# A decode block's last sum in two halves on GpSimd and VectorE, its x written by VectorE, and Wo's rows in other pieces

## Chip, cores and metric

The kernel runs on one core of one Trainium2 chip. Its time is in microseconds (us) of device time; the median of three runs before the change is 197.61 us (197.59 to 197.65). One execution was also recorded by the hardware profiler; all stage times and durations are from it.

## What is computed

One decoding step for eight sequences: a layer norm of x, attention of 32 query heads over the last 2,048 positions of a cache with 8 key and value heads, and beside it a gated unit whose result scales the attention's output.

```python
x = A_x                                    # 8 x 1 x 512
xn = layernorm(x)
W = min(4096, max(256, Sk // 4))           # 2048 of 8192
q = xn @ wq                                # 32 heads of 128
k, v = last W positions of the caches, each head for 4 query heads
p = softmax(q k * 128 ** -0.5)
s = (p v) @ wo                             # 4096 -> 512
h = sigmoid(xn @ w_gate) * (xn @ w_up)     # 512 -> 1792
g = silu(h @ w_down)                       # 1792 -> 512
return x + s * g
```

All inputs are bf16. Keys, values and weights are about 81 MB, each byte used once.

## The kernel before

**Loads.** All large loads are issued from SyncE's queue, in one list `loads` (L156 to L162): Wq, then keys and values of the eight sequences in turn, then the gate and up weights, the down weights and Wo. Each goes into one of five equal buffers (`ring`); `issue_loads` (L165) issues as many as there are free buffers and is called again whenever the code has put down the last use of one. A load into a used buffer waits on SyncE's queue for the engines that read the buffer. Each DMA also takes one of eight completion lanes in turn and waits until the lane's earlier DMA has landed.

**x.** ScalarE's queue loads x once as `x_bf`, 8 partitions of 512 (L84). For the last sum x is also wanted in another layout, `x2_sb`: columns 0 to 255 on partitions 0 to 7, columns 256 to 511 on partitions 32 to 39, zeros in the rest (L94). `load_x2` (L121), in the list behind sequence 3's first value load, makes it: GpSimd copies the first half from `x_bf` (L122), and a DMA from SyncE fetches the second half from memory (L123). It needs no ring buffer.

**Start.** VectorE does the layer norm; PE transposes it; VectorE copies it to `xnT_sb` (L210). From L213 on VectorE makes small constants from the identity, and GpSimd copies them into larger ones (L222 to L299) and clears `qz` and `o2_sb` (L305, L377). PE computes the queries (L316).

**Loop over sequences.** VectorE transposes the keys in four pieces (`k_turn`, L384), PE computes scores (L401), VectorE and ScalarE the softmax, PE spreads the probabilities (L447) and multiplies them with the values (L501), and the result goes to `o2_sb` (L552).

**End.** The gated unit (L569 to L610) leaves `gate`, 64 x 256, in the same two-part layout. Wo is loaded in pieces by rows (`load_wo`, L141): 128 partitions with 32 rows of 512 each, rows 0 to 30 in pieces of 11, 8, 6, 4 and 2 (L147) and row 31 in two halves of columns (L153). PE goes through the rows in order (`out_row`, L676), two matmuls for each of the two column halves `s`, into two PSUM tiles. After row 31's half `s` VectorE multiplies that half with `gate` into `prod` (L690). When both halves are there, one VectorE operation adds `x2_sb` (L694) and two DMAs, one each from SyncE and ScalarE, write the two halves of the columns to memory (L696).

Of the kernel before, what the change touches and what calls it, by code (L numbers as in the profile page):

```python
# [10 lines left out]
def kernel(  # L11
# [13 lines left out]
    nc = tc.nc  # L25
    P = 128
    B, _, D = A_x.shape
# [22 lines left out]
    NCOL = 2  # L50
    DC = D // NCOL
# [6 lines left out]
    bf16 = mybir.dt.bfloat16  # L58
# [3 lines left out]
    ALU = mybir.AluOpType  # L62
# [5 lines left out]
    work = ctx.enter_context(tc.tile_pool(name="work", bufs=1))  # L68
# [14 lines left out]
    x_bf = work.tile([B, D], bf16, name="x_bf")  # L83
    nc.scalar.dma_start(out=x_bf[:], in_=A_x.flatten_outer_dims())  # L84

    def ring_tile(name):
        return ring.tile([P, BIG], bf16, name=name, tag="ring", align_bytes=ALIGN)
# [5 lines left out]
    x2_sb = work.tile([NCOL * 32, DC], bf16, name="x2_sb")  # L93
# [24 lines left out]
        v_tiles[b] = t  # L118
        load_heads(t, A_v_cache, b)

    def load_x2():  # L121
        nc.gpsimd.tensor_copy(out=x2_sb[:B, :], in_=x_bf[:, :DC])  # L122
        nc.sync.dma_start(  # L123
            out=x2_sb[32 : 32 + B, :], in_=A_x.flatten_outer_dims()[:, DC:]
        )

    def load_in():
        t = ring_tile("wgu_sb")
        for n, w in enumerate((B_w_gate, B_w_up)):
            v = t[:, n * KT * F : (n + 1) * KT * F].rearrange(  # L130
                "p (kt n) -> p kt n", kt=KT
            )
            nc.sync.dma_start(out=v, in_=w.rearrange("(p kt) n -> p kt n", kt=KT))
            w_tiles["gu"[n]] = v
# [7 lines left out]
    def load_wo():  # L142
        t = ring_tile("wo_sb")
        v = t[:].rearrange("p (m n) -> p m n", m=MR)
        src = A_wo.rearrange("(p m) n -> p m n", m=MR)
        for m0, m1 in ((0, 11), (11, 19), (19, 25), (25, 29), (29, 31)):
            nc.sync.dma_start(out=v[:, m0:m1, :], in_=src[:, m0:m1, :])  # L147
        last, last_src = (
            w[:, MR - 1, :].rearrange("p (c s n) -> p s c n", c=NCOL, s=2)
            for w in (v, src)  # L150
        )
        for s in range(2):
            nc.sync.dma_start(out=last[:, s], in_=last_src[:, s])  # L153
        w_tiles["o"] = v

    loads = [(load_wq,), (load_k, 0), (load_k, 1), (load_k, 2), (load_v, 0)]  # L156
    for b in range(3, B):
        loads += [(load_k, b), (load_v, b - 2)]
        if b == 3:
            loads.append((load_x2,))  # L160
    loads += [(load_v, B - 2), (load_v, B - 1), (load_in,), (load_down,), (load_wo,)]
    free_bufs = [RING]  # L162

    def issue_loads():
        while loads:  # L165
            small_one = loads[0][0] is load_x2
            if not small_one and free_bufs[0] == 0:
                return
            f, *a = loads.pop(0)
            f(*a)  # L170
            if not small_one:
                free_bufs[0] -= 1

    issue_loads()


# [14 lines left out]
        out=rstd[:], in_=mv[:, 1:2], func=AF.Sqrt, bias=eps_t[:], scale=1.0  # L191
# [4 lines left out]
        out=xn_bf[:],  # L196
        in0=x_f[:],
# [6 lines left out]
    for kt in range(KT):  # L204
        nc.tensor.transpose(
            out=xnT_ps[:, kt, :], in_=xn_bf[:B, kt::KT], identity=ident[:B, :B]
        )
    xnT_sb = work.tile([P, KT, PW], bf16, name="xnT_sb")
    nc.vector.memzero(xnT_sb[:])
    nc.vector.tensor_copy(out=xnT_sb[:, :, :B], in_=xnT_ps[:])  # L210

    rows16 = consts.tile([P, GR], f32, name="rows16")
    nc.vector.tensor_reduce(  # L213
        out=rows16[:],
        in_=ident[:].rearrange("p (g x) -> p x g", x=GR),
        axis=AX.X,
        op=ALU.add,
    )
    rows128 = []
    for gg in range(NG):  # L220
# [3 lines left out]
            out=t[:, :, gg],  # L224
            in_=rows16[:]
# [8 lines left out]
        out=quarter[:],  # L234
        in_=ident[:].rearrange("p (h q) -> p q h", q=QP),
        axis=AX.X,
        op=ALU.add,
    )
    nc.gpsimd.tensor_copy(
        out=block[:], in_=quarter[:].unsqueeze(2).to_broadcast([P, QP, PW])  # L240
# [3 lines left out]
        out=same[:],  # L244
        in_=ident[:].rearrange("p (g j r) -> p g r j", j=QP, r=rep),
        axis=AX.X,
        op=ALU.add,
# [3 lines left out]
        out=SumM[:].rearrange("p (g j r) -> p g j r", j=QP, r=rep),  # L251
        in_=same[:]
# [6 lines left out]
        out=Jneg[:],  # L259
        in_=ident[:].rearrange("p (a j r) -> p j a r", j=QP, r=rep),  # L260
        axis=AX.XY,
        op=ALU.add,
    )
    nc.vector.tensor_scalar(
        out=Jneg[:], in0=Jneg[:], scalar1=-scale, scalar2=None, op0=ALU.mult
# [3 lines left out]
        out=Hm[:],  # L269
        in_=ident[:].rearrange("p (a gl) -> p gl a", gl=GL),  # L270
        axis=AX.X,
        op=ALU.add,
# [3 lines left out]
        out=Cm4[:],  # L276
        in_=ident[:].rearrange("p (u c x) -> p c u x", c=4, x=GR),
        axis=AX.XY,
        op=ALU.add,
# [3 lines left out]
        out=Cm2[:],  # L283
        in_=ident[:].rearrange("p (u c x) -> p c u x", c=2, x=GR),
        axis=AX.XY,
        op=ALU.add,
# [3 lines left out]
        out=heads[:], in_=same[:].unsqueeze(2).to_broadcast([P, XR, QP])  # L290
# [3 lines left out]
        out=spr[:],  # L294
        in_=ident[:].rearrange("k (gl cl p) -> k cl p gl", gl=GL, cl=CL),
    )
    quad = consts.tile([P, QP, QP, PW], bf16, name="quad")
    for a in range(QP):
        nc.gpsimd.tensor_copy(  # L299
            out=quad[:, :, a, :], in_=ident[:].rearrange("k (a w) -> k a w", a=QP)  # L300
# [10 lines left out]
    for s in range(2):  # L311
# [13 lines left out]
        for e in range(2):  # L325
            nc.vector.tensor_copy(  # L326
                out=qx_sb[:, s, :, :, e, :],
                in_=q_ps[:].rearrange(
                    "p (r wb w e) -> p e r wb w", r=rep, wb=WE // 2, e=2
                )[:, e],  # L330
            )
    free_bufs[0] += 1
    issue_loads()
    qT_sb = work.tile([P, 2 * rep * WE, PW], bf16, name="qT_sb")
    nc.vector.transpose(
        out=qT_sb[:].rearrange("p m b -> p (m b)"),
        in_=qx_sb[:].rearrange("p s r wb e w -> p (s r wb e w)"),
    )
    qc_sb = work.tile([P, GL, NG, rep, WE, B], bf16, name="qc_sb")
    for i in range(2):  # L340
        qr_ps = psum.tile([P, 2, 2 * rep * WE * B], f32, name="qr_ps", tag="o_ps")
        for aa in range(2):
# [9 lines left out]
            out=qc_sb[:, 2 * i : 2 * i + 2].rearrange("p gl g r we b -> p (gl g r we b)"),  # L352
            in_=qr_ps[:].rearrange("p a m -> p (a m)"),
# [260 lines left out]
    for b in range(B + 1):  # L614
        s = b - 1
# [24 lines left out]
        if turn:  # L640
            qk(b)
            free_bufs[0] += 1
            issue_loads()
            if s - 1 >= 0:
                for gg in range(NG):
                    pv(s - 1, gg)
        else:
            pv(s - 1, 1)
# [23 lines left out]
    prod = work.tile([NCOL * 32, DC], bf16, name="prod")  # L672

    def out_row(m, s):
        for c in range(NCOL):
            nc.tensor.matmul(  # L676
                a_ps[s][32 * c : 32 * (c + 1), :],
                lhsT=o2_sb[:, m, :],
                rhs=w_tiles["o"][:, m, DC * c + HC * s : DC * c + HC * (s + 1)],
                start=(m == 0),  # L680
                stop=(m == MR - 1),
                tile_position=(0, 32 * c),
                skip_group_check=True,
            )

    for m in range(MR):
        for s, n in enumerate(halves):
            out_row(m, s)
            if m == MR - 1:
                nc.vector.tensor_tensor(  # L690
                    out=prod[:, n], in0=gate[:, n], in1=a_ps[s][:], op=ALU.mult
                )
    y_bf = work.tile([NCOL * 32, DC], bf16, name="y_bf")
    nc.vector.tensor_tensor(out=y_bf[:], in0=prod[:], in1=x2_sb[:], op=ALU.add)  # L694
    for c in range(NCOL):
        queues[c].dma_start(  # L696
            out=out.flatten_outer_dims()[:, DC * c : DC * (c + 1)],
            in_=y_bf[32 * c : 32 * c + B, :],
# [31 lines left out]
```

## Time and profile before

| | |
|---|---|
| median of runs | 197.61 us |
| profiled execution | 197.44 us |
| span of its instructions | 195.7 us |
| PE busy | 111.6 us (57%) |
| VectorE (DVE) busy | 117.6 us (60%) |
| ScalarE (ACT) busy | 38.6 us (20%) |
| GpSimd (POOL) busy | 6.4 us (3%) |
| read from memory | 81.01 MB, 414 GB/s over the span |
| TensorE clock granted, mean | 0.813 |

Busy times are sums over an engine's instructions; engines work side by side, so they don't add up to the span. The last landing of a large load is at about 192.3 us of the span, the last arithmetic at 193.06 to 193.34, the two output DMAs are issued at 193.37. The profiled execution is 0.17 us shorter than the median of the runs and 1.74 us longer than its own span.

The first use of GpSimd is at 0.24 us, the last one ends at about 11.5 us, with the copy for `x2_sb`.

### The profile page before, as it was taken

The numbers are of one execution on the slowest core, as the hardware profiler recorded it, in microseconds if no ns is written. First come the engines' busy times: TensorE is split into PE (matmuls) and PEld (weight loads), VectorE is DVE, ScalarE is ACT, GpSimd is POOL, SyncE is SP. The second block draws the span as 40 slices with busy tenths as digits, with TensorE's granted clock in tenths as the row PEclk, the third lists the DMA queues.
The fourth block names the chain that finished last, engine by engine and source line by source line (L and its number), as shares of the span: only waits on it lengthen the run. The fifth ranks groups of instructions, "written<-read, shape, count | busy, mean of one in ns | idle before, by whom it ended". The sixth has DMA issues, their size and how long they took to land.

```text
span 195.7 us, 2620 instructions
## 1 busy us (share of the span) xinstructions
PE 111.6 (57%) x1092; PEld 44.6 (23%) x1092; DVE 117.6 (60%) x176; ACT 38.6 (20%) x112; POOL 6.4 (3%) x22
## 2 busy tenths in 40 slices
PE   0133025709809980799059914990796199684362
PEld 0011001102002240214022411150215024462351
DVE  3404498299299449935895489739936952455001
ACT  3001910015015011501141104211501110233000
POOL 2730000000000000000000000000000000000000
PEclk9999555966985996589757985699589669999998
DMA  6999999999999999999999999999999999999991
GB/s 241 457 408 442 432 429 429 429 432 425 429 429 429 427 429 429 432 424 439 432 439 422 439 435 435 429 432 425 432 429 429 425 429 429 429 431 429 416 396 41
DMA packets 6410, 81.17 MB, mean 415 GB/s; under 512 B 992, under 2 KB 1024, under 8 KB 1408
## 3 DMA queue, kind: packets, MB, share of 16 engines
q1 hardware_dynamic: 6368, 81.01, 97.2%
q8 instruction: 8, 0.13, 0.2%
q10 hardware_dynamic: 32, 0.01, 0.0%
q14 instruction: 2, 0.02, 0.0%
HBM read 81.01 MB, written 0.01 MB: 414 GB/s over the span
## 4 chain that ended last, share of the span: by engine, by line
PE 38%; DVE 35%; DMA 23%; ACT 1%; issue 1%; SPq 1%; DVEq 0%
PE s_ps L401 27%; DVE k_sb L384 27%; DMA wo_sb<-in_A_wo_dram 12%; DMA k_sb<-in_A_k_cache_dram 11%; PE o_ps L501 8%; DVE pt_bf L441 2%; DVE o_r L522 2%; PE o_ps L530 1%; DVE o_sb L552 1%; ACT o_r L518 1%; DVE o_q L543 1%; DVE mx L414 1%; PE a_ps L676 1%; SPq L147 0%; SPq L101 0%
## 5 line engine op out<-in xcount | busy, mean ns | idle before, releaser
L384 DVE STREAM_TRANSPOSE k_sb<-k_sb 128x2048 uint32<-128x2048 uint32 x32 | 72.9, 2291 | 5.7 <-DMA k_sb<-in_A_k_cache_dram 5.7
L401 PE MATMUL s_ps<-k_sb,qz 128*32 128x512 bf16 x256 | 61.6, 1086 | 11.8 <-DVE k_sb L384 11.5
L447 PE MATMUL pc_ps<-pt_bf,spr 128*32 128x128 bf16 x128 | 4.7, 292 | 40.7 <-DVE pt_bf L441 40.7
L414 DVE TENSOR_REDUCE mx<-s_ps 128x1 f32<-128x512 f32 x8 | 5.5, 691 | 29.0 <-PE s_ps L401 29.0
L501 PE MATMUL o_ps<-v_sb,pT_sb 128*32 128x256 bf16 (+1 forms) x416 | 21.0, 298 | 0.0
L401 PEld LDWEIGHTS <-qz 128*32 128x32 bf16 x256 | 8.8, 115 | 49.8 <-issue 49.7
L501 PEld LDWEIGHTS <-pT_sb 128*32 128x32 bf16 (+1 forms) x416 | 14.0, 101 | 14.5 <-issue 9.9
L362 ACT COPY qz<-qc_sb 32x64 bf16<-32x64 bf16 x64 | 16.4, 302 | 0.7
L518 ACT ACTIVATE o_r<-o_ps,Cm 128x128 f32<-128x128 f32 x16 | 5.9, 368 | 52.0 <-PE o_ps L501 52.0
L522 DVE SCALAR_TENSOR_TENSOR o_r<-o_ps,Cm,o_r 128x128 f32<-128x128 f32 x28 | 9.7, 350 | 9.8 <-ACT o_r L518 9.3
L428 ACT ACTIVATE p_bf<-s_ps,nm 128x512 bf16<-128x512 f32 x8 | 5.5, 687 | 49.7 <-DVE nm L425 49.7
L447 PEld LDWEIGHTS <-spr 128*32 128x32 bf16 x128 | 3.4, 121 | 41.4 <-issue 40.7
L530 PE MATMUL o_ps<-o_r,rows 128*128 128x128 f32 x32 | 7.5, 320 | 4.8 <-DVE o_r L522 4.8
L483 DVE TENSOR_SCALAR pT_sb<-pc_bf,Hm 128x512 bf16<-128x512 bf16 x32 | 9.0, 352 | 0.2 <-ACT pc_bf L457 0.2
L457 ACT CAST pc_bf<-pc_ps 128x512 bf16<-128x512 f32 x8 | 4.7, 586 | 20.3 <-PE pc_ps L447 20.3
L316 PE MATMUL q_ps<-wq_sb,xnT_sb 128*32 128x512 bf16 x32 | 3.8, 626 | 6.8 <-DMA wq_sb<-in_A_wq_dram 6.5
L676 PE MATMUL a_ps<-wo_sb,o_sb 128*32 128x128 bf16 x128 | 4.6, 219 | 3.9 <-DMA wo_sb<-in_A_wo_dram 3.9
L530 PEld LDWEIGHTS o_ps<-o_r,rows 128*128 128x128 f32 x32 | 4.8, 189 | 6.7 <-DVE o_r L522 6.7
L326 DVE CAST qx_sb<-q_ps 128x256 bf16<-128x256 f32 x4 | 1.5, 420 | 7.7 <-PE q_ps L316 7.7
L441 DVE STREAM_TRANSPOSE pt_bf<-p_bf 128x512 bf16<-128x512 bf16 x8 | 5.4, 675 | 0.9 <-ACT p_bf L428 0.9
L543 DVE SCALAR_TENSOR_TENSOR o_q<-o_ps,rden,block 128x128 f32<-128x128 f32 x8 | 2.8, 351 | 4.7 <-PE o_ps L530 4.7
L690 DVE TENSOR_TENSOR prod<-gate,a_ps 64x128 bf16<-64x128 f32 x2 | 0.5, 279 | 7.5 <-PE a_ps L676 7.5
(64 smaller groups left out, 56.2 us busy)
## 6 DMA issues: line engine op xcount, KB each, us to landing
k_sb<-in_A_k_cache_dram SPq DMA_DIRECT2D x8, 4096.0 KB, 29.9
v_sb<-in_A_v_cache_dram SPq DMA_DIRECT2D x8, 4096.0 KB, 23.4
wq_sb<-in_A_wq_dram SPq DMA_DIRECT2D x1, 3072.0 KB, 11.6
wgu_sb<-in_B_w_gate_dram SPq DMA_DIRECT2D x1, 1792.0 KB, 25.1
wgu_sb<-in_B_w_up_dram SPq DMA_DIRECT2D x1, 1792.0 KB, 28.9
wd_sb<-in_B_w_down_dram SPq DMA_DIRECT2D x1, 1792.0 KB
wo_sb<-in_A_wo_dram SPq DMA_DIRECT2D x1, 1408.0 KB
wq_sb<-in_A_wq_dram SPq DMA_DIRECT2D x1, 1024.0 KB
```

The lines of the kernel that those rows point to most:

```text
L362: nc.scalar.copy(out=z[rows, GL * gg : GL * (gg + 1), :, c0 : c0 + rep], in_=qc_sb[rows, :, gg, :, :, b].rearrange("p gl r we -> p gl we r"),)
L384: nc.vector.transpose(out=words, in_=words)
L401: nc.tensor.matmul(s_tiles[b][PW * gl : PW * (gl + 1), :], lhsT=qz[b % 2][:, h, we, :], rhs=kv[:, gg, gl, we // 2, we % 2], start=(we == 0 ...
L414: nc.vector.reduce_max(out=mx[:], in_=s_tiles[b][:], axis=AX.X)
L441: nc.vector.transpose(out=pt_bf[:].rearrange("p c g a r -> p (c g a r)"), in_=p_bf[:])
L447: nc.tensor.matmul(pc_ps[PW * a : PW * (a + 1), cl], lhsT=spr[:, cl].rearrange("k p gl -> k (p gl)"), rhs=pt_bf[:, :, :, a, :], start=True ...
L483: nc.vector.tensor_scalar(out=pT[:, :, :, gl, :], in0=pc[:].rearrange("p c g r -> p g c r"), scalar1=Hm[:, gl : gl + 1], scalar2=None, op0 ...
L501: nc.tensor.matmul(o_ps[rows * cg : rows * (cg + 1), :], lhsT=pT_tiles[b][:, gg, nch * m : nch * (m + 1)].rearrange("p c g r -> p (c g r)" ...
L518: nc.scalar.activation(out=o_r[:], in_=o_ps[:, 0:Dh], func=AF.Copy, scale=cm[:, 0:1])
L522: nc.vector.scalar_tensor_tensor(out=o_r[:], in0=o_ps[:, Dh * c : Dh * (c + 1)], scalar=cm[:, c : c + 1], in1=o_r[:], op0=ALU.mult, op1=AL ...
L530: nc.tensor.matmul(o2_ps[:], lhsT=rows128[gg][:].rearrange("p gl g r q -> p (gl g r q)"), rhs=o_r[:], start=(gg == 0), stop=(gg == NG - 1),)
L676: nc.tensor.matmul(a_ps[s][32 * c : 32 * (c + 1), :], lhsT=o2_sb[:, m, :], rhs=w_tiles["o"][:, m, DC * c + HC * s : DC * c + HC * (s + 1)] ...
```

## The change

- `load_x2` is gone, with its DMA, its GpSimd copy and its place in the list; `issue_loads` loses the case for it.
- VectorE writes both parts of `x2_sb` from `x_bf`, two copies of 8 x 256 bf16 behind the copy to `xnT_sb`.
- Wo's rows 0 to 30 come in pieces of 7, 7, 6, 5, 4 and 2. Row 31's two halves stay.
- The last sum is done by halves, each behind its product: the first half by GpSimd, the second by VectorE. The two output DMAs still write one half of the result's columns each, from other partitions, and so each needs both halves of the sum.

```diff
-    def load_x2():
-        nc.gpsimd.tensor_copy(out=x2_sb[:B, :], in_=x_bf[:, :DC])
-        nc.sync.dma_start(
-            out=x2_sb[32 : 32 + B, :], in_=A_x.flatten_outer_dims()[:, DC:]
-        )
...
-        for m0, m1 in ((0, 11), (11, 19), (19, 25), (25, 29), (29, 31)):
+        for m0, m1 in ((0, 7), (7, 14), (14, 20), (20, 25), (25, 29), (29, 31)):
             nc.sync.dma_start(out=v[:, m0:m1, :], in_=src[:, m0:m1, :])
...
-        if b == 3:
-            loads.append((load_x2,))
...
-        while loads:
-            small_one = loads[0][0] is load_x2
-            if not small_one and free_bufs[0] == 0:
-                return
+        while loads and free_bufs[0]:
             f, *a = loads.pop(0)
             f(*a)
-            if not small_one:
-                free_bufs[0] -= 1
+            free_bufs[0] -= 1
...
     nc.vector.tensor_copy(out=xnT_sb[:, :, :B], in_=xnT_ps[:])
+
+    for c in range(NCOL):
+        nc.vector.tensor_copy(
+            out=x2_sb[32 * c : 32 * c + B, :], in_=x_bf[:, DC * c : DC * (c + 1)]
+        )
...
+    y_bf = work.tile([NCOL * 32, DC], bf16, name="y_bf")
+    adders = [nc.gpsimd, nc.vector]
     for m in range(MR):
         for s, n in enumerate(halves):
             out_row(m, s)
             if m == MR - 1:
                 nc.vector.tensor_tensor(
                     out=prod[:, n], in0=gate[:, n], in1=a_ps[s][:], op=ALU.mult
                 )
-    y_bf = work.tile([NCOL * 32, DC], bf16, name="y_bf")
-    nc.vector.tensor_tensor(out=y_bf[:], in0=prod[:], in1=x2_sb[:], op=ALU.add)
+                adders[s].tensor_tensor(
+                    out=y_bf[:, n], in0=prod[:, n], in1=x2_sb[:, n], op=ALU.add
+                )
```

## The prediction

> **What bounds the kernel now.** I read the slices of the page first, then the DMA queues, the tail in stages, the chain of waits, and last the tail in order of time.
>
> The DMA row of the 40 slices and two rows of the queues (packets, MB, share of 16 engines):
>
> ```profile
> DMA  6999999999999999999999999999999999999991
> ...
> q1 hardware_dynamic: 6368, 81.01, 97.2%
> q8 instruction: 8, 0.13, 0.2%
> ```
>
> The DMA engines are never idle between about 2 us and 190 us: 81 MB go through one queue. No computation sets the length of this kernel before its last stage; what counts is how much work each DMA engine has, and what follows the last byte. The tail by stages (busy time of PE, PEld, DVE, ACT, POOL, then clock, DMA share, GB/s):
>
> ```profile
> 188.00:190.00 2.00, 1.07 (x32) 0.93 (x32) 0.00 (x0) 0.00 (x0) 0.00 (x0) 1.00 1.01 409
> 190.00:191.00 1.00, 0.85 (x24) 0.71 (x24) 0.00 (x0) 0.00 (x0) 0.00 (x0) 1.00 0.85 281
> 191.00:192.00 1.00, 0.67 (x18) 0.53 (x19) 0.00 (x0) 0.00 (x0) 0.00 (x0) 1.00 0.57 162
> 192.00:193.00 1.00, 0.65 (x12) 0.39 (x11) 0.49 (x2) 0.00 (x0) 0.00 (x0) 1.00 0.00 0
> ```
>
> The share falls from 1.01 to 0.85 and 0.57 before the transfers end at 192.0: some engines finish over a microsecond before the slowest, and a piece has landed only when the slowest has done its part. The end of the chain of waits (start, us, what) and the issues of the last two pieces:
>
> ```profile
> 167.94 23.33 DMA wo_sb<-in_A_wo_dram
> 191.27 0.04 issue
> 191.32 0.62 PE a_ps L676 x16
> 191.94 0.01 issue
> 191.95 0.50 PE a_ps L676 x10
> 192.45 0.02 issue
> 192.47 0.51 DVE prod L690 x2
> 192.98 0.03 DVEq L694
> 193.01 0.04 issue
> 193.06 0.28 DVE y_bf L694
> ```
>
> ```profile
> L153 SPq DMA_DIRECT2D wo_sb<-in_A_wo_dram x2: 374/378/383, 173.9 to 178.1; - x2
> ...
> DMA to landing us min/median/max: 14.2/16.3/18.3
> ```
>
> Rows 25 to 28 of Wo land at 191.27, the first half of row 31 at 173.9 + 18.3 = 192.2, the second at 178.1 + 14.2 = 192.3. PE has the first half's sum 0.25 us later and the two products follow at once. So the path is: last transfers, two matmuls, prod, prod, y_bf, out. In order of time:
>
> ```profile
> 192.47 0.49 DVE L690 TENSOR_TENSOR prod<-gate,a_ps 64x128 bf16<-64x128 f32 x2 [7.48 <-PE a_ps L676]
> 193.06 0.28 DVE L694 TENSOR_TENSOR y_bf<-prod,x_sb 64x256 bf16<-64x256 bf16 x1
> 193.37 0.32 SPq L696 DMA_DIRECT2D out_dram<-y_bf  x1
> ```
>
> **Start.** Two VectorE copies of 8x256 bf16 are added behind L210. No row has this shape: bounds are the 128x32 copy (175 ns) and the 8x512 cast (415 ns). I take 0.2 us each, 0.4 together. Behind them on VectorE stand the constants L213 to L282, which end at 7.57 and would end at 7.97; VectorE's next work is at 14.32, when PE has the first query sums. GpSimd waits for L213 and ends its setup at 11.2; it would end at 11.6, less the 0.39 us of the copy L122 that is gone. The first readers of what it makes are PE at 18.2 (quad) and ScalarE at 19.8 (qz). Over 6 us of cover: 0.0 us. Without it, up to 0.8.
>
> **SyncE's queue.** The issue L123 (0.53 us at 38.7) goes; the next issue waits until 52.98 anyway. Nothing. The completion lanes are handed out in turn, eight of them, so one small load less and one piece more changes what the late pieces wait for: now row 31's halves wait for the gate and up weights (173.9, 178.1); in the changed program rows 29 and 30 wait for gate, the halves for up and down. The last half is thus issued when the down weights land, at 182.4, not at 178.1. Its turn on the engines comes near 191.8, and the first x load took under 2 us from issue (0.73) to its reader (2.66). Cover 7 us: 0.0.
>
> **Wo's pieces.** Rows 0 to 24 come in four pieces instead of three; the cut at 25 and everything behind it stay. Earlier first rows let PE begin earlier, but PE sits waiting four times for pieces (3.9 us in all), and what it waits for last, rows 25 to 28, is behind the same bytes. No gain. The price is one piece more: 128 packets and 16 semaphore packets, eight and one per engine. In the trace's packet records a packet takes 84 ns at 2,048 bytes, 159 at 4,096, 309 at 8,192, and 9 at 4 bytes: 9 ns fixed. So 9 x 9 = 81 ns on each engine. The x load that goes had a packet of 27 ns and a semaphore of 9 on eight of the 16. Net +0.045 or +0.081: I take +0.06. Bounds: the pieces of 1,024, 768 and 512 KB were followed by PE 2.36, 1.85 and 1.25 us after the piece before, a straight line with 0.14 us at no bytes, so +0.14 above; below, -0.04, if packets overlap fully and only the load's removal counts.
>
> **The sum in halves.** VectorE's f32 TENSOR_TENSORs take 279 ns for 128 columns and 411 for 256: 147 fixed. y_bf of 256 bf16 columns takes 284, so 137 for columns; with 128, 147 + 69 = 0.215 us. It starts 0.03 to 0.08 us behind the second prod (192.98) and ends by 193.28, against 193.34.
>
> GpSimd's half waits for the first prod, done at 192.47 + 0.28 = 192.75. L223 on GpSimd started 0.15 us after its releaser L213 ended (5.93 to 6.08), so it starts at 192.90. No row has a two-input operation on GpSimd. Below: the 128-column copy, 0.29 us. Above: two of the slow 128-column copy L293 (391 ns), 0.78. The row nearest to it is the copy of 8x256 bf16, which also reads 256 bf16 values a partition: 386 ns. I take 0.39, which ends at 193.29 (193.19 to 193.68). Both output DMAs then wait for both engines; SyncE started 0.03 us after VectorE, and after GpSimd I take 0.08 (0.03 to 0.15). Out is issued at 193.37, as before: 0.00 us, with -0.06 (VectorE's own half) and +0.46 as bounds. Behind that wait stands nothing but the end of the program.
>
> [...]
>
> **Sum.** 0.0 + 0.0 + 0.06 + 0.00 = +0.06 us. The profiled execution: span 195.7 and 1.74 around it, 197.44; it becomes 197.50. The median of the runs, 197.61, stands 0.17 higher, so 197.67. A measurement of this kernel can tell about 0.2% from no change, 0.4 us: 197.2 to 198.0.
>
> **The rivals.**
>
> *The two halves don't run side by side* (the change does not do what it says). Both adds read two operands from SBUF. If VectorE's half has to wait for GpSimd's, it starts at 193.29 + 0.03, ends at 193.54, and out goes at 193.57: +0.20, with the piece +0.26, so 197.87. For it: nothing in the trace excludes it, since no two-input VectorE operation from SBUF runs beside GpSimd (GpSimd is done at 11.2 us). Against it: the one-input VectorE copy SumM at 6.35 (226 ns) ran across GpSimd work without visible delay. [...]
>
> *GpSimd's add is long* (slower than before). It is GpSimd's first work after 181 us, of a kind it has not run. At 0.78 us, with the late handover of 0.15, out goes at 193.83: +0.46 and the piece, +0.52, so 198.13. It decides from an add of about 0.65 us. For it: the spread of GpSimd's copies at 128 columns, 291 to 391 ns. Against it: the first copy L223 took 236 ns, the second as much.
>
> *The slowest DMA engine changes* (faster). Equal bytes go to all engines, yet they end over 1 us apart; the eight 16 KB instruction packets of q8 (a data packet of 16,384 bytes takes 611 ns) are the work that isn't equal. If these fall otherwise over the engines, the last transfer ends up to 0.61 us earlier and all behind it too: 197.67 - 0.61 = 197.06. It counts as faster from 0.46 us. For it: the falling share from 190 on. Against it: PE's program, which q8 feeds, keeps its 2,090 instructions. The reverse, 198.28, is as likely.
>
> **How the numbers follow.** Forecast (197.67) 0.48; halves in turn (197.87) 0.28; long add (198.13) 0.12; engines earlier 0.06, later 0.06. The first two are within 0.2%: same 0.76; faster 0.06; slower 0.12 + 0.06 = 0.18. Range: down to 197.40 (both lower bounds give 197.51, and a little of the earlier engines), up to 198.15, which takes in the long add.
>
> **What would show it.** Right: y_bf on GpSimd starts near 192.9 and lasts about 0.4 us, VectorE's half starts within 0.1 us of the second prod, out goes within 0.1 us of 193.37, rows 25 to 28 land 0.0 to 0.15 later. Wrong: VectorE's half starts only when GpSimd's ends; GpSimd's add over 0.65 us; last landings moved by over 0.2 us; PE waiting for row 31's second half. If PE's last wait ends before the first of these landings, the reading of the path is wrong.

## The result, and the profile after

| | before | changed |
|---|---|---|
| median of runs | 197.62 us (197.53 to 197.67, 8 runs) | 198.34 us (197.93 to 198.80, 8 runs) |
| profiled execution | 197.44 us | 198.06 us |
| its span, and what lies around it | 195.74 + 1.70 us | 196.27 + 1.79 us |

The ratio is 1.0035, 95% interval 1.0026 to 1.0044: 0.72 us slower, above the top of the range (198.15). In later series of runs, beside other kernels, the changed kernel had 198.00 against 197.59, 1.0022 [1.0014, 1.0031]. What lies around the span before is 1.70 us; the 1.74 ahead of the prediction came from the span rounded to 195.7.

First the page of the changed kernel: the row of the DMA share in 40 slices and that of the data queue (packets, MB, share of 16 engines).

```profile
DMA  6999999999999999999999999999999999999990
...
q1 hardware_dynamic: 6496, 81.01, 97.0%
```

The engines are as full as before; the queue has 6,496 packets for 6,368: 144 more for the piece, 16 fewer for the load of x that is gone. The tail in stages (columns as in the prediction):

```profile
190.00:191.00 1.00, 0.71 (x20) 0.60 (x20) 0.00 (x0) 0.00 (x0) 0.00 (x0) 1.00 0.85 299
191.00:192.00 1.00, 0.49 (x18) 0.46 (x16) 0.00 (x0) 0.00 (x0) 0.00 (x0) 1.00 0.58 173
192.00:193.00 1.00, 0.82 (x18) 0.43 (x12) 0.26 (x2) 0.00 (x0) 0.00 (x0) 1.00 0.05 11
```

The share falls as it did before (0.85 and 0.58, for 0.85 and 0.57), but in the last stage 0.05 is left where there was 0.00: the last bytes come later. The last steps of the chain of waits, and then the same place in order of time:

```profile
174.10 18.10 DMA wo_sb<-in_A_wo_dram
...
192.24 0.47 PE a_ps L669 x10
...
192.74 0.49 DVE prod L685 x2
```

```profile
192.74 0.48 DVE L685 TENSOR_TENSOR prod<-gate,a_ps 64x128 bf16<-64x128 f32 x2 [7.15 <-PE a_ps L669]
193.10 0.42 POOL L688 TENSOR_TENSOR y_bf<-prod,x_sb 64x128 bf16<-64x128 bf16 x1 [181.79 <-DVE prod L685]
193.26 0.34 DVE L688 TENSOR_TENSOR y_bf<-prod,x_sb 64x128 bf16<-64x128 bf16 x1
193.66 0.36 SPq L692 DMA_DIRECT2D out_dram<-y_bf  x1
```

The first `prod` starts at 192.74 instead of 192.47, and from there to the issue of the output it takes 0.92 us instead of 0.90. GpSimd's add lasts 0.42 us, VectorE's half 0.34 instead of the 0.215 that was worked out, and both end within 0.1 us of each other. So the sum in halves, on which the prediction spent its rivals, changed almost nothing.

The span is 0.53 us longer: 0.27 until `prod`, 0.02 in the sum, and 0.24 behind the issue of the output, where the prediction had "nothing but the end of the program". Around the span there are 0.09 us more. The end of the program is a few rows of the last source line. Each engine has `DRAIN` rows there, called drains below, and `EVENT_SEMAPHORE` rows, where the engines meet: a first meeting, a last drain, a last meeting. For that line, before and then changed (engine, operation, count, duration in ns as min/median/max, first and last start in us):

```profile
L725 PEldq DRAIN  x2: 13/148/282, 192.4 to 195.3; - x2
L725 DVEq DRAIN  x2: 19/158/297, 193.1 to 195.2; - x2
```

```profile
L721 PEldq DRAIN  x2: 13/148/283, 192.7 to 195.6; - x2
L721 DVEq DRAIN  x2: 138/260/382, 193.3 to 195.9; - x2
```

PE's last drain starts 0.3 us later than before, with everything else. VectorE's last drain comes 0.7 us later: before it started beside PE's, now 0.3 us behind it, and the last meeting of the engines waits for it: in the instruction records before, all drains have ended by 195.42 and the other engines' last meeting rows start at 195.54 to 195.60; in the changed kernel VectorE's drain ends at 196.06, all others by 195.74, and the other engines' last rows start at 196.17 to 196.22. VectorE has no work of the program left there. This is what the experiments had to explain.

### The profile page after: what moved, and what is told of

It is laid out like the page before. It is cut to its first block, busy times and chain, and to the rows that moved or that the text cites. A ratio compares the mean times of both kernels' runs of the same rounds, so it can differ in the third digit from the quotient of the medians.

```text
span 196.3 us, 2621 instructions
## 1 busy us (share of the span) xinstructions
PE 114.5 (58%) x1092; PEld 47.7 (24%) x1092; DVE 118.1 (60%) x178; ACT 38.6 (20%) x112; POOL 6.5 (3%) x22
## 3 DMA queue, kind: packets, MB, share of 16 engines
q1 hardware_dynamic: 6496, 81.01, 97.0%
## 4 chain that ended last, share of the span: by engine, by line
PE 36%; DMA 33%; DVE 28%; issue 1%; ACT 1%; SPq 0%; DVEq 0%
PE s_ps L394 25%; DVE k_sb L377 21%; DMA wgu_sb<-in_B_w_gate_dram 13%; DMA k_sb<-in_A_k_cache_dram 11%; DMA wo_sb<-in_A_wo_dram 9%; PE o_ps L494 7%; DVE o_r L515 2%; DVE pt_bf L434 2%; PE o_ps L523 1%; PE pc_ps L440 1%; PE den_ps L459 1%; DVE o_sb L545 1%; ACT o_r L511 1%; DVE o_q L536 1%; DVE mx L407 1%
## 5 line engine op out<-in xcount | busy, mean ns | idle before, releaser
L494 PE MATMUL o_ps<-v_sb,pT_sb 128*32 128x256 bf16 (+1 forms) x416 | 22.8, 321 | 0.0
L394 PEld LDWEIGHTS <-qz 128*32 128x32 bf16 x256 | 10.1, 115 | 48.8 <-issue 48.6
L494 PEld LDWEIGHTS <-pT_sb 128*32 128x32 bf16 (+1 forms) x416 | 15.2, 108 | 14.8 <-issue 9.7
L523 PE MATMUL o_ps<-o_r,rows 128*128 128x128 f32 x32 | 8.6, 361 | 4.6 <-DVE o_r L515 4.4
L523 PEld LDWEIGHTS o_ps<-o_r,rows 128*128 128x128 f32 x32 | 5.5, 222 | 6.7 <-DVE o_r L515 6.3
```

The costliest lines, as they stand in the source:

```text
L394: nc.tensor.matmul(s_tiles[b][PW * gl : PW * (gl + 1), :], lhsT=qz[b % 2][:, h, we, :], rhs=kv[:, gg, gl, we // 2, we % 2], start=(we == 0 ...
L494: nc.tensor.matmul(o_ps[rows * cg : rows * (cg + 1), :], lhsT=pT_tiles[b][:, gg, nch * m : nch * (m + 1)].rearrange("p c g r -> p (c g r)" ...
L523: nc.tensor.matmul(o2_ps[:], lhsT=rows128[gg][:].rearrange("p gl g r q -> p (gl g r q)"), rhs=o_r[:], start=(gg == 0), stop=(gg == NG - 1),)
```

## The experiments

Each kernel was timed in 10 or 11 runs (the one with eleven pieces in 6), beside 21 to 33 runs of the kernel before, whose median was 197.59 to 197.62 each time; kernels of different series are compared through it. A time is the median, with the range in brackets.

### The parts one by one

One piece more, in the kernel before:

```diff
-        for m0, m1 in ((0, 11), (11, 19), (19, 25), (25, 29), (29, 31)):
+        for m0, m1 in ((0, 7), (7, 14), (14, 20), (20, 25), (25, 29), (29, 31)):
```

> The kernel before with Wo's rows in the six new pieces, nothing else changed. Theory D (the transfers: one more piece, and row 31's second half issued only when the down weights have landed, cost the 0.28 us by which row 31 landed later, and make the runs differ among themselves): 197.9 to 198.1 median, runs spread over 0.4 us or more, last piece's landing near 192.45. Theory G (the cost is at the end, GpSimd's add and what follows it): 197.65 to 197.7, spread under 0.2 us. Theory S (the last transfers end at a time that depends on which DMA engines the instruction packets fall on, any edit moves it): any value, with the last landing moved by 0.2 us or more either way.

Measured: 197.78 (197.71 to 197.96), 1.0010 [1.0001, 1.0018], +0.16 us with an interval of 0.02 to 0.36.

The x for the sum by VectorE alone; pieces and sum as before:

```diff
-            loads.append((load_x2,))
...
+    for c in range(NCOL):
+        nc.vector.tensor_copy(
+            out=x2_sb[32 * c : 32 * c + B, :], in_=x_bf[:, DC * c : DC * (c + 1)]
+        )
```

> Only x2_sb written by VectorE and its load removed; old pieces, old sum by VectorE in one. Theory D: as before, 197.55 to 197.65, spread under 0.2 us. Theory G: as before too. Theory S: last landing moved by 0.2 us or more, time with it.

Measured: 197.99 (197.85 to 198.14), 1.0018 [1.0009, 1.0027], +0.37 us. This is the part with the largest price, and the prediction put it at 0.0.

The sum in halves alone:

```diff
-    nc.vector.tensor_tensor(out=y_bf[:], in0=prod[:], in1=x2_sb[:], op=ALU.add)
+                adders[s].tensor_tensor(
+                    out=y_bf[:, n], in0=prod[:, n], in1=x2_sb[:, n], op=ALU.add
+                )
```

> Only the sum in halves, the first by GpSimd; x2_sb and pieces as before. Theory G: 198.0 to 198.4, with the spread of the changed kernel; in the profile VectorE's half ends 0.05 to 0.1 us after GpSimd's, and 0.2 to 0.3 us more pass between the issue of the output and the end than in the kernel before. Theory D: within 0.05 us of before, because prod to output issue was 0.90 us before and 0.92 us in the changed kernel. Theory S: last landing moved.

Measured: 197.79 (197.67 to 197.89), 1.0007 [0.9998, 1.0016]. In its profile the first `prod` to the issue of the output takes 0.98 us for 0.90: +0.08.

The changed kernel with both halves of the sum on VectorE:

```diff
-    adders = [nc.gpsimd, nc.vector]
+    adders = [nc.vector, nc.vector]
```

> The changed kernel with both halves added by VectorE: product, sum, product, sum in its queue. Theory G: back to 197.6 to 197.75, spread under 0.2 us. Theory D: 197.9 to 198.2, the spread of the changed kernel remains. By the rows: two sums of 0.215 us in place of one of 0.284, with one more hand-over, so prod to output issue 0.90 + 0.1 to 0.2 us.

Measured: 197.97 (197.61 to 198.21), 1.0016 [1.0007, 1.0025]. Its sum in order of time:

```profile
192.93 0.22 DVE L688 TENSOR_TENSOR y_bf<-prod,x_sb 64x128 bf16<-64x128 bf16 x1
...
193.38 0.22 DVE L688 TENSOR_TENSOR y_bf<-prod,x_sb 64x128 bf16<-64x128 bf16 x1
```

The same operation on the same shape lasts 0.22 us, as worked out, when GpSimd isn't adding beside it, and 0.34 in the changed kernel. From the first `prod` to the output it is 1.01 us here, so GpSimd's add saves 0.08. What was lost isn't there.

Of the three accounts in these expectations, D (the transfers) wanted 197.9 to 198.1 from the pieces alone and no change from x alone, and G (the end of the sum) 198.0 to 198.4 from the halves alone and 197.6 to 197.75 without GpSimd's add. All four came out otherwise. S (the last transfers move with any edit) stays open: the last data packet ends at 192.20 to 192.43 in these four profiles and at 192.03 in that of the kernel before, which is the earliest of all.

### Is it the copies' work, or that they are there?

The copies end at 5.66 us; GpSimd's setup ends at 11.3, and its readers wait until 18 us, as forecast. So their 0.43 us is covered, and what remains is that VectorE's program has other instructions. The trace records 192 instructions of VectorE and its queue before, and 193 in the changed kernel: two copies more, and one semaphore wait less ahead of the sum (the `DVEq` step at 192.98 in the chain shown in the prediction; x is now VectorE's own). The experiments that follow change this number and nothing that counts in time.

The changed kernel again, for a second median and profile:

> The changed kernel once more, beside the three that follow. Theory F (the end barrier of the program waits for VectorE's 192nd recorded instruction, 0.48 us after the one before it, as if its code had to be fetched; in the kernel before that is the very last instruction, in the changed kernel the one before the last barrier step): 198.2 to 198.4, VectorE's last drain 0.48 us after the barrier step ahead of it. Theory N (the 0.7 us are mostly session noise and runs that differ): 197.8 to 198.1.

Measured: 198.00 (197.91 to 198.59), 1.0022 [1.0014, 1.0031].

The changed kernel with one memset of 8 x 1 on VectorE ahead of the constants (194 instructions):

```diff
+    pad0 = work.tile([B, 1], f32, name="pad0")
+    nc.vector.memset(pad0[:], 0.0)
```

> The changed kernel with one more VectorE instruction at the start (a memset of 8x1, read by nothing), 194 in all. Theory F: the 192nd is now an instruction that waits for the barrier anyway, so the stall disappears: 0.3 to 0.4 us faster than the changed kernel of the same call, the pause of 0.48 us gone from the end. Theory N, or any theory in which the sum or the transfers are the whole cause: no change, within 0.1 us.

Measured: 197.99 (197.61 to 198.23), 1.0018 [1.0009, 1.0027]. The median didn't gain the 0.3 to 0.4 us that account F (the pause at the 192nd instruction) wanted; four of the ten runs, at 197.61 to 197.76, come near it.

The kernel before with two such memsets (194):

> The kernel before with two such memsets on VectorE, 194 instructions. Theory F: 0.1 us faster than before (197.5), since its last instruction no longer comes 0.12 us behind those of the other engines. Theory N: within 0.05 us of before.

Measured: 197.74 (197.52 to 198.09), 1.0010 [1.0001, 1.0019]. The gain of 0.1 us that was expected didn't come.

The kernel before with one such memset (193):

> The kernel before with one such memset, 193 instructions as in the changed kernel, and nothing else changed. Theory F: 0.2 to 0.3 us slower than before (197.8 to 197.95), with the drain late as in the changed kernel. Theory N: within 0.05 us of before.

Measured: 197.92 (197.80 to 198.21), 1.0018 [1.0009, 1.0027], +0.33 us. A memset of 8 values at the start, in an engine that then waits for PE until 14 us, costs as much as the two copies. In the instruction records (us) one finds where:

```
VectorE's recorded instructions    191st starts   192nd starts   8,192-byte packet
before (192)                       195.240        195.718        196.40
changed (193)                      195.441        195.918        196.59
before, one memset (193)           195.308        195.788        196.43
changed, both halves VectorE (194) 193.396        195.673        194.80
before, two memsets (194)          193.254        195.568        194.69
```

In the first three the 192nd follows the 191st after 0.48 us, and so it does in all twelve profiles with 192 or 193 instructions. With 193 the 192nd is the drain before the last meeting. It has nothing to wait for, and all wait for it; in the profiles with 191, 194 or 209 instructions VectorE makes the same step in 0.11 to 0.12 us. With 192 the 192nd is the last of the program, VectorE's part in the last meeting, and the pause shows little: before, it starts 0.12 us after the latest of the others. With 194 it lies behind the first meeting, where VectorE waits for two us anyway (195.6 in the table is that wait). The last column is a packet of 8,192 bytes on the queue that the profile calls q14, instruction. It starts 1.1 to 1.5 us behind the 191st in all five.

The price can be read in every profile, from the output's issue to the end of the timed execution: 4.07 to 4.20 us in the six with 192, 4.35 to 4.46 in the six with 193, whatever else was changed in them, and 4.35 to 4.37 in the three with 194. These three profiles are of runs a little above their kernels' medians, and the median of the kernel before with two memsets is only 0.15 us up. What costs something with 194 isn't as clear: the packet comes beside the output's own transfer, and the first meeting comes 2.03 to 2.04 us after the output's issue, in all others 1.74 to 1.89.

What VectorE does in these 0.48 us is not shown. That it waits for a fetch of its instructions, and that the packet is VectorE's, is the author's reading, from the packet of 8,192 bytes that comes 1.1 to 1.5 us after the 191st and moves with VectorE's instructions; no run measured a fetch.

### Fewer, and many more

If the place of the 192nd decides, fewer or many more must help. The changed kernel with two VectorE instructions less, the layer norm reading `x_bf` without a cast and one constant set by GpSimd (191):

```diff
-    nc.vector.tensor_copy(out=x_f[:], in_=x_bf[:])
...
-    nc.vector.bn_stats(out=stats[:], in_=x_f[:])
+    nc.vector.bn_stats(out=stats[:], in_=x_bf[:])
...
-    nc.vector.memset(eps_t[:], 1e-5)
+    nc.gpsimd.memset(eps_t[:], 1e-5)
```

> The changed kernel with two VectorE instructions fewer at the start: the layer norm reads x_bf directly, without the cast to x_f, and eps_t is set by GpSimd. 191 on VectorE, so none is the 192nd. Theory F (VectorE's 192nd instruction waits 0.48 us for its code): 0.35 us faster than the changed kernel, 197.6 to 197.7, no pause in the end barrier and no instruction packet beside the output's transfer. Theory without it: 197.95 to 198.05, as the changed kernel of the call before.

Measured: 197.86 (197.74 to 198.11), 1.0014 [1.0005, 1.0024]: 0.14 us under the changed kernel, where 0.35 was expected.

The same two less in the kernel with x by VectorE alone (191):

> x_sb written by VectorE, old pieces, old sum, and the same two instructions fewer: 191. Theory F: 0.12 us less than before for the missing pause and 0.08 us less between the first product and the output's issue (one wait fewer before the sum): 197.4. Theory without it: as the kernel with x_sb by VectorE alone, 197.95 to 198.0.

Measured: 197.79 (197.67 to 197.90), 1.0010 [1.0001, 1.0019].

The kernel before with `eps_t` set by GpSimd, one less (191):

> The kernel before with eps_t set by GpSimd, 191 instructions on VectorE. Theory F: 0.12 us faster than before, 197.45 to 197.5. Theory without it: as before, within 0.05 us.

Measured: 197.72 (197.61 to 198.34), 1.0007 [0.9998, 1.0016]. The gains over the kernel before that were expected of these two didn't come. In all runs but one their spans are no longer than before's (195.7 to 196.0), but 1.93 to 1.94 us lie around the spans of the three profiles with 191, instead of 1.70 to 1.73. The reading that fits is that the pause has left the span and stands behind it; the packet comes at 197.0 to 197.5, after the last recorded instruction.

Sixteen memsets more in the changed kernel (209), and in the one with x by VectorE alone (209):

```diff
+    pad = work.tile([B, 16], f32, name="pad")
+    for i in range(16):
+        nc.vector.memset(pad[:, i : i + 1], 0.0)
```

> The changed kernel with sixteen 8x1 memsets on VectorE at the start, read by nothing: 209 on VectorE, so the 192nd comes some 16 instructions ahead of the end, near 173 us, where VectorE has time. Theory F (its code is waited for): no pause at the end and no instruction packet beside the output: 0.3 us faster than the changed kernel, 197.65 to 197.75. If the pause costs nothing: as the changed kernel, 198.0.

> x_sb by VectorE alone, with the same sixteen memsets. Theory F: no pause, and one wait fewer before the sum: 197.4 to 197.5, faster than before by 0.1 to 0.2 us. Without theory F: 197.95 to 198.0, as x_sb by VectorE alone.

Measured: 197.78 (197.67 to 197.98), 1.0009 [1.0000, 1.0018], and 197.75 (197.48 to 198.36), 1.0008 [0.9999, 1.0017]. Sixteen instructions more make the changed kernel 0.2 us faster; the two other changed kernels of the same series, with 193, had 197.97 and 198.02 (below). The second was expected at 197.4 to 197.5, under the kernel before, and isn't. The packet is at 161.2 us now, while VectorE waits for PE's scores, and the end has no pause. It isn't at the 192nd instruction any more: only 176 of VectorE's have started by then. So 192 holds for these kernels of 191 to 194 instructions; it is not a fixed place in every program.

The sharpest pair came last: `eps_t` set by GpSimd and nothing else, which gives 192 in each. The kernel with x by VectorE alone:

```diff
-    nc.vector.memset(eps_t[:], 1e-5)
+    nc.gpsimd.memset(eps_t[:], 1e-5)
```

> x_sb by VectorE alone, with eps_t set by GpSimd: 192 instructions on VectorE as in the kernel before, so the same small pause as there, and 0.08 us less between the first product and the output's issue. Theory F: 197.5 to 197.6, level with before or 0.08 us faster. If writing x_sb by VectorE costs something itself: as the kernel with it alone, 197.95 to 198.0.

Measured: 197.66 (197.47 to 197.75), 1.0001 [0.9992, 1.0010], where it had 197.99 with 193. The 0.08 us that the shorter wait before the sum should gain over the kernel before don't show.

And the changed kernel:

> The changed kernel with eps_t set by GpSimd, 192 on VectorE, everything else as changed. Theory F: 0.25 to 0.35 us faster than the changed kernel: 197.7 to 197.75, which is one piece (0.1 us) and 0.02 us of the sum above before. Without it: 198.0.

Measured: 197.71 (197.62 to 198.00), 1.0008 [0.9999, 1.0017], where it had 198.00. The rows of its last line:

```profile
L721 PEldq DRAIN  x2: 13/148/282, 192.5 to 195.5; - x2
L721 DVEq DRAIN  x2: 19/200/380, 193.1 to 195.4; - x2
```

VectorE's last drain starts beside PE's again. One memset on another engine is worth 0.3 us here, and the x by VectorE costs nothing that can be measured once the count is 192. It is not the memset's own work: the same move gained nothing in the kernel before (197.72). None of the kernels tried beats the kernel before.

### Why VectorE's half is slow

VectorE's half with x taken from PSUM, where ScalarE puts it at the start, so that one of its two operands isn't in SBUF:

```diff
+    x2_ps = psum1.tile([NCOL * 32, DC // 2], f32, name="x2_ps", tag="x2_ps")
+    nc.scalar.copy(out=x2_ps[:], in_=x2_sb[:, DC // 2 :])
...
-                    out=y_bf[:, n], in0=prod[:, n], in1=x2_sb[:, n], op=ALU.add
+                    out=y_bf[:, n],
+                    in0=prod[:, n],
+                    in1=x2_sb[:, n] if s == 0 else x2_ps[:],
+                    op=ALU.add,
```

> The changed kernel with x's second half also copied to PSUM by ScalarE at the start, and VectorE's half of the sum read from there: one operand from SBUF in place of two. Lock theory (two operands from SBUF hold up VectorE while GpSimd adds): VectorE's half lasts 0.28 us, the duration of this form in prod, and ends before GpSimd's or with it; the output is issued 0.05 to 0.1 us earlier after prod. If VectorE's 0.35 us come from something else: it stays at 0.33 us or more.

Measured: 197.97 (197.90 to 198.34), 1.0021 [1.0012, 1.0030], no change in the time. The sum in order of time:

```profile
193.45 0.42 POOL L690 TENSOR_TENSOR y_bf<-prod,x_sb 64x128 bf16<-64x128 bf16 x1 [181.89 <-DVE prod L687]
193.60 0.28 DVE L690 TENSOR_TENSOR y_bf<-prod,x_ps 64x128 bf16<-64x128 bf16 x1
```

The half ends at 193.88, at GpSimd's end (193.87); in the changed kernel it ended 0.08 us after it. It takes the 279 ns that the products with an operand in PSUM take, and `prod` to output is 0.85 us for 0.92. So with both operands in SBUF VectorE's half was held up beside GpSimd's add, as the first rival has it, by 0.07 us against this form; what holds it up is not recorded. The other profiles bear it out: in all eight with a GpSimd add and both of VectorE's operands in SBUF, VectorE's half lasts 0.336 to 0.355 us and ends 0.081 to 0.082 us after GpSimd's, however long it lasted.

### Pieces and the clock

Six pieces more in the kernel before, to get the price of one:

```diff
-        for m0, m1 in ((0, 11), (11, 19), (19, 25), (25, 29), (29, 31)):
+        for m0, m1 in ((0, 3), (3, 6), (6, 9), (9, 12), (12, 15), (15, 18),
+                       (18, 20), (20, 23), (23, 25), (25, 29), (29, 31)):
```

> The kernel before with Wo's rows 0 to 30 in eleven pieces instead of five; the cut at row 25 and what follows stay, VectorE keeps 192 instructions. Six pieces more at 81 ns on every DMA engine: +0.49 us, 198.05 to 198.15, and the last transfer as much later. If packets overlap and a piece costs nothing: within 0.1 us of before. If a piece costs what the six-piece kernel showed, 0.16 us: +1.0 us.

Measured: 198.19 (197.87 to 198.58, 6 runs), 1.0030 [1.0018, 1.0042]: +0.58, 0.10 us a piece.

Part of that may be the clock. In its profile the granted clock is half from 191.2 us to the end, and in three profiles of kernels with six pieces it is half in the last stage too. The changed kernel with one memset, in stages:

```profile
190.00:191.00 1.00, 0.56 (x12) 0.56 (x13) 0.00 (x0) 0.00 (x0) 0.00 (x0) 0.50 0.90 314
191.00:192.00 1.00, 1.00 (x25) 0.99 (x21) 0.00 (x0) 0.00 (x0) 0.00 (x0) 0.50 0.57 168
```

PE is busy for the whole of 191 to 192 where it needed half of it, is behind the transfers, and its first `prod` starts at 192.88. In three other profiles with six pieces it starts at 192.60 to 192.65, and their last data packets end at 192.14 to 192.20, for 192.16 here.

That the pieces bring this about isn't shown. Of nine profiles of kernels with six pieces three have the half clock in the last stage, of nine with five pieces none, which chance alone could give. Spells of half clock come in every profile, and late ones with five pieces too: from 183.5 to 190.3 us in the kernel with the sum in halves alone. To keep PE from pausing, seven matmuls into an unused tile were put ahead of four rows of Wo in the changed kernel:

```diff
+        for _ in range({7: 2, 14: 2, 20: 2, 25: 1}.get(m, 0)):
+            nc.tensor.matmul(
+                fill_ps[:],
+                lhsT=xnT_sb[:, 0, :],
+                rhs=w_tiles["d"][:, 0, :],
...
+            )
```

> The changed kernel with seven matmuls of 512 columns into an unused PSUM tile, in PE's gaps ahead of rows 7, 14, 20 and 25. Theory C (smaller pieces leave PE idle more evenly, the granted clock falls to 0.5 in some executions' last microseconds and PE becomes the end): the clock stays 1.0 to the end, runs spread under 0.3 us, median at most 198.0, without the runs at 198.3 and more. Without theory C: median and spread as the changed kernel, 198.0 (197.9 to 198.6), or later by what the filling costs.

Measured: 198.02 (197.89 to 198.18), 1.0021 [1.0011, 1.0030]. The clock in its profile is 1.00 to the last meeting, as in six of the nine without the filling, so the profile alone decides nothing. None of its eleven runs is above 198.18, where eight of the changed kernel's nineteen were, in other series. The median stays.

The runs without a profile give a hint. Of the four kernels with six pieces that have no pause before the last meeting, three (191, 192 and 209 instructions) have together eight runs with a mean granted clock of 0.843. They took 198.06 to 198.11, 197.98 to 198.00 and 197.94 to 197.98 us in that order, 0.16 to 0.29 above their kernels' medians. The one of them with a profile has the clock at 0.50 from 189.1 to 192.5 us. Two runs of the kernel before with the same mean took 197.55 and 197.61.

## Why the prediction was wrong

**The step that failed** is "Start", with its "Over 6 us of cover: 0.0 us", and with it the sentence that nothing but the end of the program stands behind the output. The cover was there and held: 0.43 us of copies measured for 0.4, and no reader waited. But the copies were priced by their duration alone, and the waits that they save weren't counted at all. Two instructions more and one less put VectorE's 0.48 us pause before the engines' last meeting. In place of 0.0 the runs show 0.33 (one memset in the kernel before), 0.33 (x by VectorE, 193 to 192 instructions) and 0.29 (changed, 193 to 192). That is some 0.3 of the 0.72 us; the later series, with 0.41 over the kernel before, is this and the piece. What made the first series 0.34 longer still is open (below).

**The pieces**: +0.06 forecast; +0.16 [0.02, 0.36] and 0.10 a piece measured. The 81 ns of each engine's packets would be most of it. Half clock in the last stage wasn't in the sum; that the piece brings it is not shown.

**The sum in halves**: 0.00 forecast, +0.02 measured, by errors that cancel. That is luck. GpSimd started 0.09 us behind its product (0.15 forecast) and took 0.42 (0.39 forecast). VectorE's half took 0.34 (0.215), and the wait before the sum is one shorter, which the kernel with x by VectorE alone shows as 0.82 us for 0.90.

**The rivals.** That VectorE's half is held up beside GpSimd's add is right in kind and was too dear at 0.20: GpSimd's add starts before VectorE's second product ends and VectorE's half ends 0.08 us behind it, not 0.25, so VectorE loses 0.07 against the form with one operand in PSUM: its half took 0.34 us with both in SBUF, 0.28 with one in PSUM. The long add isn't so: 0.42 us after 181 us of rest. That another DMA engine becomes the slowest is not seen, as the share of the DMA falls in the same way (and the records hold 2,194 instructions of PE, weight loads and queue included, before and after, not 2,090), but later transfers aren't excluded: the last data packet ends 0.30 us later than in the profile before, over the 0.2 that the prediction named as a sign of being wrong. By its own measure of 0.4 us the result is "slower", to which it gave 0.18, and for other causes.

**The sum of it.** The changed kernel with 192 instructions had seven of its eleven runs at 197.62 to 197.72, with a median of 197.65: 0.05 above the kernel before, where +0.06 was forecast. Eight of the eleven runs with 193 lie at 197.91 to 198.06, median 197.97: 0.32 more, the pause. Both groups were picked after the runs were seen; over all runs it is 0.11 and 0.29. Of the four runs above with 192, two have the mean clock of 0.843; of the slower ones with 193 none has it. In the first series five of eight runs are such slower ones (198.25 to 198.80), in the second three of eleven. Why it was five, and up to 0.8 us, stays open: the one profile of that series, 198.06, has the full clock. The transfers can do it too. The profile of the kernel before with one instruction less happens to be of a run at 198.34, 0.62 above its median: its clock is full in the last stage, 24.35 MB had landed on the data queue at 60 us where 24.61 had in the kernel before, and its last data packet ends at 192.72. How much of the 0.27 us to the first `prod` is real stays open as well: the kernel before's own profile, with its last data packet at 192.03, is the earliest of all (192.05 to 192.72 in the others) and 0.17 us under the median of its runs.

## What to carry to other kernels

Here one 8 x 1 memset that nothing reads put a pause of 0.48 us on VectorE where all engines wait for it, and the median rose by 0.33 us. When a change of a few tenths of a us has no visible place, look at the rows of the last drains and meetings first, and try one idle instruction more or less: it costs one run and separates the edit's work from its place. Medians of such differences hide groups of runs; look at the single runs and their clocks before the difference is put down to one cause.

## What the runs showed of the hardware

- In kernels with 192 or 193 recorded VectorE instructions the 192nd starts 0.48 us after the 191st, in all twelve profiles, and a packet of 8,192 bytes follows. With 193 this step is the one from the first meeting to the last drain, which takes 0.11 to 0.12 us in the profiles with 191, 194 or 209. One 8 x 1 memset in a kernel of 197.6 us cost 0.33 us for that; sixteen more gave 0.2 back in the changed kernel.
- What lies around the span isn't fixed: 1.70 to 1.73 us with 192 instructions on VectorE, 1.78 to 1.82 with 193, 194 or 209, 1.93 to 1.94 with 191.
- A VectorE add with both operands in SBUF (64 x 128, bf16) takes 0.22 us alone and ended 0.08 us after the GpSimd add that ran beside it in all eight profiles; with one operand in PSUM it took 0.28.
- The granted clock of TensorE fell to 0.50 between 189.0 and 191.2 us in three of nine profiles of kernels with six pieces. PE was busy for 0.96 of the 2.00 us from 186 to 188 in these three, with pauses of 0.3 to 1.1 us between the pieces from there on; it was 0.96 in three of the other six too.
